# A two-pass order for a planned kernel: the first layout's times, shifted for 116 groups of operations, rank the second, and ten groups of keys are added in one VectorE sum

## The chip, the cores and the metric

The kernel runs on one core of one Trainium2 chip. The metric is the device time of one execution in microseconds. The instructions of each engine (TensorE, shown as PE for products and PEld for weight loads; VectorE as DVE; ScalarE as ACT; GpSimd as POOL; SyncE as SP, which issues the transfers) stand in one fixed order, written when the kernel is built, and an engine executes them strictly in that order. What another engine or a transfer has to deliver is waited for at the instruction that needs it.

## The reference

Four residual blocks on x of 2048 rows by 640 columns: attention, MLP, attention, MLP, both pairs with the same weights.

```python
def A(x, wqkv, wo):                    # 32 heads of 20 columns
    q, k, v = split(x @ wqkv)
    idx = pos[:, None] - arange(8) * 2 # 8 keys per row, every second row back
    logits = where(idx >= 0, einsum(q, k[idx]) * 20 ** -0.5, -1e9)
    return einsum(softmax(logits), v[idx]) @ wo
def B(x, w1, b1, w2, b2):              # 640 -> 1536 -> 640
    return gelu(layernorm(x) @ w1 + b1) @ w2 + b2
x = x + A(layernorm(x)); x = x + B(layernorm(x))
x = x + A(layernorm(x)); x = x + B(layernorm(x))
```

## The kernel before

**Units.** The 2048 rows are cut into four units of 512 rows (even and odd rows apart, since keys stand two rows back), four tiles of 128 rows each. Two layers make eight units, n = 0 to 7. A float32 factor is held as two float16 parts, the high part and what is left, and a product of two such factors is three TensorE products (`PASS`). The left-over part costs one subtraction: `yl` for layer norm rows, `lo` for weights, `hlo` for the MLP's hidden values, `ol` for attention's result. ScalarE makes the high part before it (`yh`, `hi`, `hhi`, `oh`).

**A unit's path.** Layer norm (`layernorm`); rows split and transposed by a DMA into `yT`; QKV products (`qkv`, for units 4 to 7 `qkv7`, with seven instead of eight half-size products, in steps P1 to P7 with ScalarE copies between them); results written to DRAM (`spill`) and read back as windows (`fetch`); attention on VectorE (`attention`); its output transposed and multiplied by wo (`project`); a second layer norm; the MLP (`mlp`, 12 blocks e of 128 hidden columns: `hp` is the first product of a block, `outh` and `out` the second). The last two units' MLP is done together (`pair`).

**Attention on VectorE.** A unit has four groups of 8 heads, so there are 32 groups G. A group runs products of q and its 8 keys (`qk`, L1004, 5120 elements a partition), the sum over a head's columns (`lg`, L1009), mask, maximum, difference, exponent on ScalarE, sum (`s`), reciprocal (`rc`), weights (`at`), products with v (`pv`, L1026), and then the sum over the 8 keys in three additions of 2560, 1280 and 640 elements (`ad`, twice L1031, and `o`, L1034).

**Weights.** While unit 0's MLP runs, the 12 blocks of W1 and W2 are loaded (`st`, L531), scaled and split (`sc` L539, `hi` L540, `lo` L541) and stored for later units (`mw`, L551). W2's blocks stand in three buffers c2: a block takes one for the loaded float32 values and one for its two parts, which is free again when the block's products and its store are done. Units 4 to 7 need combined blocks of the QKV weights, built by `factors` (`fr` loads, L764; `fs` four differences, L772; `fh`, `fl`).

**The planner.** `Plan.add` collects some 3,700 operations with an engine, a cost, a priority, what they need and give, and the buffers they use. `Plan.run` lays them out in time: of the operations that are ready on an engine, the one with the least key (earliest start, then priority, then number) is next. The result is only the order; the chip sets the times. An operation added with `either` (rather than `dve`) may go to GpSimd instead of VectorE, but only where the plan has VectorE in an `lg` sum: the planner opens such a stretch (`open_`) at every `lg` and puts the operation there if it fits. `HOLD` keeps an `either` operation from VectorE for some time, so that such a stretch may come. The lines that set a pick:

```python
key = (max(t - o["wait"], clock[e] + 0.05, (o["born"] + o["hold"]) * (e == "dve" and o["hold"] > 0)), o["prio"], o["n"])
```

Of the kernel before, what the change touches and what calls it, by code (L numbers as in the profile page):

```python
# [37 lines left out]
FAST = ([0, 1, 2], [0, 1])  # L38
# [29 lines left out]
PAIRS = ("qk", "pv", "ad", "o", "sub", "at", "hlo", "yl", "xb", "ol", "wq", "lo", "lm")  # L68

HOLD = {'lo': 0, 's': 2, 'hlo': 0, 'b': 0, 'xb': 20, 'ol': 12, 'ol3': 0}  # L70
# [3 lines left out]
QKV_AT = (-500, -499, 0, 9, 9, 6, 4, 0)  # L74
ROWS_AT = (-500, -199, -198, -17, -16, -15, -94, -13)
INNER_AT = (-150, -149, -698, -147, -146, -145, -694, -43)
HOLD_A = (0, 6, 6, 12, 12, 6, 0, 12)
PREP_AT = 0
# [7 lines left out]
class Plan:  # L86
# [12 lines left out]
    REACH = 0.75  # L99
# [11 lines left out]

    def __init__(self, slots):
        self.ops = []
        self.free = {pool: [(0.0, i) for i in range(n)] for pool, n in slots.items()}
        self.users = {}
        self.slot = {}
        self.since = {}
        self.last = {}
        self.turn = {}
        self.line = {}  # L120
        self.turns_up = {}

    def add(self, eng, dur, prio, emit, need=(), give=(), use=(), table=None, move=None, lazy=False, wait=None,
# [3 lines left out]
                 wait=self.PATIENCE * (eng == "dve" and prio < -200) if wait is None else wait)  # L127
        self.ops.append(o)
        for u in use:
            if u not in self.users and u[0] in self.ORDERED and u not in self.line.setdefault(u[0], []):  # L130
                self.line[u[0]].append(u)
            self.users[u] = self.users.get(u, 0) + 1

    def run(self):
        when = {}
# [115 lines left out]
        while len(order) < total:  # L251
            best = None
            for e, ops in ready.items():
                pick = None
                for o in ops:
# [3 lines left out]
                    key = (max(t - o["wait"], clock[e] + 0.05, (o["born"] + o["hold"]) * (e == "dve" and o["hold"] > 0)), o["prio"], o["n"])  # L259
# [66 lines left out]
def sliding_dilated_then_mlp_kernel(  # L326
# [121 lines left out]
    def either(n, hold, prio, emit, need=(), give=(), use=(), aside=None):  # L448
        dve(n, prio, emit, need, give, use, aside=aside or 0.12 + n / 500.0, hold=hold)
# [218 lines left out]
    def sums_of_rows(n, prio, name, yk, lk, col):  # L668
# [4 lines left out]
        for b in range(2):  # L673
# [9 lines left out]
            def sum1(yks=yks):  # L683
                y1 = tile_of(*yks[1])
                nc.vector.tensor_add(y1[:, :KQ], y1[:, :KQ], y1[:, KQ:2 * KQ])

            def sums(yks=yks):
                y0, y1 = (tile_of(*k) for k in yks)
                nc.vector.tensor_sub(y0[:, :KQ], y1[:, :KQ], y0[:, :KQ])
# [55 lines left out]
    def flat(t):  # L745
        return t.rearrange("p k a c -> p (k a c)")
# [864 lines left out]
```

## Time and profile before

| | |
|---|---|
| median of 3 runs | 1133.01 us (1132.67 to 1134.62) |
| the profiled execution's own time | 1132.52 us |
| its span, first to last instruction | 1130.7 us |
| mean granted TensorE clock | 0.998 |
| TensorE products | 6536, busy 1118.3 us, 99% of the span |
| VectorE | busy 1050.9 us, 93% |
| ScalarE, GpSimd | busy 672.8 us (59%) and 144.6 us (13%) |
| moved by DMAs | 250.91 MB |

The time of a run is the span and some 1.8 us around it (1132.52 less 1130.7). A busy share says how much of the span an engine had an instruction in work, not whether that work set the end; a matmul's end is modelled in these records, so TensorE's pace is read from the starts of groups of equal products.

### The profile page before, as it was taken

The numbers are of one execution on the slowest core, as the hardware profiler recorded it, in microseconds if no ns is written. First come the engines' busy times: TensorE is split into PE (matmuls) and PEld (weight loads), VectorE is DVE, ScalarE is ACT, GpSimd is POOL, SyncE is SP. The second block draws the span as 40 slices with busy tenths as digits, with TensorE's granted clock in tenths as the row PEclk, the third lists the DMA queues.
The fourth block names the chain that finished last, engine by engine and source line by source line (L and its number), as shares of the span: only waits on it lengthen the run. The fifth ranks groups of instructions, "written<-read, shape, count | busy, mean of one in ns | idle before, by whom it ended". The sixth has DMA issues, their size and how long they took to land.

```text
span 1130.7 us, 17031 instructions
## 1 busy us (share of the span) xinstructions
PE 1118.3 (99%) x6536; PEld 602.0 (53%) x6536; DVE 1050.9 (93%) x885; ACT 672.8 (59%) x1241; POOL 144.6 (13%) x109
## 2 busy tenths in 40 slices
PE   9999999999999999999999999999999999999998
PEld 6444455445545455455545554446445555654476
DVE  7899999999999999999999999999999998768972
ACT  6558446566946556565735675378644843858630
POOL 1102103101012013120211200112100300000000
PEclk9999999999999999999999999999999999999999
DMA  9998787689997798688785859768898766695202
GB/s 310 316 323 235 217 224 174 236 304 274 292 320 239 192 288 240 198 222 223 221 274 181 214 166 269 245 224 199 184 297 239 216 196 171 182 258 154 65 24 70
DMA packets 262605, 250.91 MB, mean 222 GB/s; under 512 B 154412, under 2 KB 219260, under 8 KB 262524
## 3 DMA queue, kind: packets, MB, share of 16 engines
q1 hardware_dynamic: 262524, 249.83, 75.6%
q8 instruction: 51, 0.84, 0.3%
q14 instruction: 30, 0.25, 0.1%
HBM read 161.49 MB, written 52.64 MB: 189 GB/s over the span
## 4 chain that ended last, share of the span: by engine, by line
PE 68%; DVE 19%; issue 5%; DMA 4%; SPq 2%; ACT 2%; POOL 0%; DVEq 0%; ACTq 0%; POOLq 0%
PE acc L1151 15%; PE ps L1130 15%; PE ps L910 13%; PE ps L838 10%; PE ps L1063 6%; PE acc L1332 3%; DVE pr L1031 3%; PE ps L1367 3%; DVE pr L1026 3%; DVE pr L1004 3%; DVE sm L1009 2%; PE ps L1332 2%; DMA c<-in_B_w_dram 1%; DVE w L654 1%; DVE act L1141 1%
## 5 line engine op out<-in xcount | busy, mean ns | idle before, releaser
L1151 PE MATMUL acc<-c,act 128*128 128x512 f16 (+1 forms) x1728 | 250.4, 300 | 3.2 <-ACT c L540 2.8
L1130 PE MATMUL ps<-yT,c 128*128 128x512 f16 x1080 | 243.7, 379 | 0.1
L1151 PEld LDWEIGHTS <-act 128*128 128x128 f16 x1728 | 136.8, 98 | 114.7 <-issue 5.3
L910 PE MATMUL ps<-wq,yT 128*128 128x480 f16 (+1 forms) x990 | 196.5, 360 | 0.6 <-ACT wq L506 0.5
L1004 DVE TENSOR_TENSOR pr<-qk 128x5120 f32<-128x5120 f32 x32 | 175.1, 5473 | 1.5 <-DMA qk<-spill 1.2
L1026 DVE TENSOR_TENSOR pr<-sm,v 128x5120 f32<-128x5120 f32 x32 | 175.7, 5490 | 0.8
L1009 DVE TENSOR_REDUCE sm<-pr 128x256 f32<-128x5120 f32 x32 | 175.1, 5472 | 0.0
L1130 PEld LDWEIGHTS <-c 128*128 128x128 f16 x1080 | 103.6, 98 | 122.0 <-DVE c L541 0.6
L910 PEld LDWEIGHTS <-yT 128*128 128x128 f16 x990 | 95.3, 98 | 99.1 <-issue 0.7
L1031 DVE TENSOR_TENSOR pr<-pr 128x2560 f32<-128x2560 f32 x64 | 137.7, 2151 | 0.1
L1063 PE MATMUL ps<-wo,yT 128*128 128x320 f16 x960 | 132.0, 299 | 0.0
L838 PE MATMUL ps<-wq,yT 128*128 128x480 f16 x528 | 112.6, 366 | 1.8 <-ACT ps L856 1.8
L1063 PEld LDWEIGHTS <-yT 128*128 128x128 f16 x960 | 93.8, 98 | 37.7
L1136 ACT ACTIVATE act<-ps,b 128x512 f32<-128x512 f32 x72 | 49.2, 684 | 83.4 <-PE ps L1130 83.0
L847 ACT ACTIVATE ev<-ps 128x480 f32<-128x480 f32 x96 | 52.8, 566 | 72.6 <-PE ps L838 67.2
L621 POOL TENSOR_TENSOR ln<-ln,half 128x2 f32<-128x2 f32 (+1 forms) x32 | 52.4, 1638 | 315.2 <-ACT ln L618 315.2
L838 PEld LDWEIGHTS <-yT 128*128 128x128 f16 x528 | 51.1, 98 | 55.8 <-issue 2.3
L930 ACT ACTIVATE ev<-ps 128x480 f32<-128x480 f32 x64 | 36.3, 569 | 73.0 <-PE ps L910 72.5
L838 PE MATMUL ps<-wq 128*128 128x480 f16 x336 | 71.8, 366 | 1.1 <-ACT ev L847 1.1
L1042 POOL TENSOR_TENSOR ohl<-w,ohl 128x640 f16<-128x640 f32 x18 | 25.3, 1403 | 296.6 <-DVE sm L1024 56.1
L1139 ACT ACTIVATE act<-act 128x512 f16<-128x512 f32 x72 | 44.8, 622 | 21.2 <-PE acc L1151 20.9
L838 PEld LDWEIGHTS <-wq 128*128 128x128 f16 x336 | 32.6, 98 | 35.7 <-issue 1.5
(224 smaller groups left out, 1323.4 us busy)
## 6 DMA issues: line engine op xcount, KB each, us to landing
c<-mw SPq DMA_DIRECT2D x126, 320.0 KB, 3.6
spill<-ev SPq DMA_DIRECT2D x64, 480.0 KB, 4.1
qk<-spill SPq DMA_DIRECT2D x32, 880.0 KB, 5.9
v<-spill SPq DMA_DIRECT2D x32, 880.0 KB, 4.9
qk<-spill SPq DMA_DIRECT2D x32, 320.0 KB, 3.3
c<-in_B_w_dram SPq DMA_DIRECT2D x24, 320.0 KB, 4.9
mw<-c SPq DMA_DIRECT2D x24, 320.0 KB, 4.6
pr<-in_B_w_dram SPq DMA_DIRECT2D x24, 320.0 KB, 3.9
```

What stands on the lines that cost most here:

```text
L621: pool(0.6, prio, lambda t0=t0, t1=t1: nc.gpsimd.tensor_tensor(col(2)[:, t0:t1], col(2)[:, t0:t1], half[:, t0:t1], op=OP.pow), need=[("vr" ...
L838: nc.tensor.matmul(ps, r(x_, j), w[:, j, y_], start=start and i == 0, stop=i == len(todo) - 1, skip_group_check=True)
L847: act(C, -400 + n, lambda: nc.scalar.activation(to(), tile_of(*bank)[:, :C].rearrange("p (a c) -> p a c", a=3), AF.Copy, scale=1.0 / WS), ...
L910: nc.tensor.matmul(ps, transposed(yk)[:, a * KD + k, t * P:(t + 1) * P], wq[:, g, k, b, i0 * GC:i1 * GC], start=first and j == 0, stop=las ...
L1004: nc.vector.tensor_mul(pr.rearrange("p w t c -> p w (t c)"), w[:, HALO + m:HALO + 2 * m].rearrange("p t c -> p (t c)")[:, None, :].to_broa ...
L1009: dve(E, G - 0.7, lambda: nc.vector.tensor_reduce(by_key(), heads(), axis=AX.X, op=OP.add), need=[("qk", G)], give=[("lg", G)], use=[*pk, sk])
L1026: dve(E, G - 0.85, lambda: nc.vector.tensor_mul(heads(), by_key()[:, :, :, None].to_broadcast([P, W, m * GH, DH]), windows(tile_of(*vw), [ ...
L1031: dve(m * w * GC, G - 0.9, lambda w=w: nc.vector.tensor_add(pr[:, 0:w], pr[:, 0:w], pr[:, w:2 * w]), need=[last], give=[("ad", G, w)], use=vk)
L1063: nc.tensor.matmul(tile_of(*pk)[:, :D // 2], transposed(yk)[:, a * KD + k, t * P:(t + 1) * P], wo[:, b, k, c * D // 2:(c + 1) * D // 2], s ...
L1130: nc.tensor.matmul(tile_of(*pk)[:, :nt], tile_of(*ck)[:, a, k * P:(k + 1) * P], transposed(yk)[:, c * KD + k, t0 * P:t1 * P], start=i == 0 ...
L1151: nc.tensor.matmul(accs[k][:, c0:c0 + n], tile_of(*hk)[:, a, (i - t0) * P:(i - t0 + 1) * P], tile_of(*wk)[:, c, w0:w0 + n], start=first, s ...
L1332: nc.tensor.matmul(tile_of(*to(i))[:, :HALF], hl()[:, a, i * P:(i + 1) * P], row(c), start=start and (a, c) == PASS[0], stop=(a, c) == PAS ...
```

## The change

**Two layouts.** `run` now calls `lay` twice. The first layout is made as before, by priorities. `rank` keeps each operation's time in it (`first`). In the second layout the rank of an operation is that time, plus a shift for its name from the table `SHIFT`: 116 names, of one operation (`'yl a 1 0'`) or of a family (`'lo m 9'`), shifted by between -206.5 and 90.5. For held operations the hold becomes "not before 3 us ahead of its rank".

**More for GpSimd.** The row sums of `sums_of_rows` (L685, and its second part), the differences of `factors` (L772) and the addition `ea` of `qkv7` (L870) become `either` operations. The list `PAIRS` and some numbers (`HOLD`, `QKV_AT`, `ROWS_AT`, `INNER_AT`, `HOLD_A`, `PREP_AT`, `REACH`) are changed. `FAST` loses its second entry: two tiles of unit 1's layer norm go from VectorE (`bn_stats`) to ScalarE.

**One sum over the keys.** For the ten groups marked in `ONCE` (1, 2, 6, 7, 9, 10, 13, 21, 30, 31) the three additions over keys become one VectorE reduction of 5120 elements to 640, read with the eight keys innermost, 2560 bytes apart (`ow`). The planner opens a stretch for GpSimd at an `ow` too.

```diff
-FAST = ([0, 1, 2], [0, 1])
+FAST = ([0, 1, 2],)
...
+SHIFT = {
+    'P7 4': -2, 'XP1 0 1': 3, 'XP1 2 1': 20, 'ad 15': 10, 'ad 17': -7, 'ad 25': 2, 'ad 25 2': 3, 'at 6': -10, 'c1 P1 3': -5, 'e 26': -17, 'fl 1': 9.5,
...
     def run(self):
+        self.lay()
+        if SHIFT:
+            self.rank()
+            self.lay()
+        return self.order
+
+    def rank(self):
+        for o in self.order:
+            o["first"] = o["at"]
...
+            if "first" in o:
+                o["rank"] = o["first"] + sum(SHIFT.get(k, 0.0) for k in set(o["key"]))
+                o["until"] = o["rank"] - self.EARLY if o["hold"] > 0 else 0.0
...
-                    key = (max(t - o["wait"], clock[e] + 0.05, (o["born"] + o["hold"]) * (e == "dve" and o["hold"] > 0)), o["prio"], o["n"])
+                    held = (o["until"] if "first" in o else o["born"] + o["hold"]) if e == "dve" and o["hold"] > 0 else 0.0
+                    key = (max(t - o["wait"], clock[e] + 0.05, held), o["rank"], o["n"])
...
-                if kind == "lg":
+                if kind in ("lg", "ow"):
                     open_.append((t, t + d))
...
-            dve(KQ, prio, sum1, need=[("y", name, 2 * b + 1)], give=[("rs", name, b)], use=held)
+            either(KQ, HOLD["rs"], prio, sum1, need=[("y", name, 2 * b + 1)], give=[("rs", name, b)], use=held)
...
+        if ONCE[G]:
+            dve(E, G - 0.9, lambda: nc.vector.tensor_reduce(
+                ot().rearrange("p t c -> p (t c)"), pr.rearrange("p w t c -> p (t c) w"), axis=AX.X, op=OP.add),
+                need=[last], give=[("ow", G), ("o", G)], use=[*vk, ok])
+        else:
...
```

The program has the same 6536 products and the same transfers on SP's queue as before, in another order. VectorE has 65 instructions fewer, GpSimd 34 more, and ScalarE 13 more, among them two more changes of its function table there and back. Ten `tensor_reduce` stand for thirty additions; moved from VectorE to GpSimd, net, are 12 of the `hlo` (L1141), 7 of the `lo` (L541), 6 `ea` (L870), 4 `yl` of units 4 to 7 (L714), one `fs` of four differences (L772), 4 first row sums (L685) and 2 other `yl` (L654); back to VectorE come 3 additions of b2 (L660) and 1 `ol` (L1042).

Three places in the order follow. Line numbers of the changed kernel differ: L579 is the weight load L531, L812 is L764, L1176 is L1123, L704 is L656, L1010 is L962, L599 is L551, L589 is L541, L1194 is L1141, L1095 is L1042, L1079 the new reduction.

SP's queue, before, from the loads for `factors` (L764) over the loads of W2's blocks 9 (into c22) and 10 (into c20); c10 to c12 are the buffers of W1's blocks, v0 and qk0 the attention's windows, yT1 transposed rows:

```order
L764 DMA wq_101<-in_A_wqkv_dram 128x3x160 x4
L1123 DMA c10_76<-mw00_110 128x1280
L962 DMA v0_68<-spill01_135 128x1760
L551 DMA mw18_130<-c20_79 128x1280
L531 DMA c22_81<-in_B_w2_dram 128x640
L551 DMA mw011_121<-c12_78 128x1280
L1123 DMA c11_77<-mw01_111 128x1280
L656 DMA_TRANSPOSE yT1_73<-w3_85 128x10x128
L1123 DMA c12_78<-mw02_112 128x1280
L531 DMA c20_79<-in_B_w2_dram 128x640
```

The same stretch of SP's queue now, to the load of block 10 (into c21):

```order
L1010 DMA v0_68<-spill01_135 128x1760
L599 DMA mw010_120<-c10_76 128x1280
L704 DMA_TRANSPOSE yT1_73<-w4_86 128x10x128
L704 DMA_TRANSPOSE yT1_73<-w3_85 128x10x128
L579 DMA c22_81<-in_B_w2_dram 128x640
L599 DMA mw18_130<-c21_80 128x1280
L1176 DMA c10_76<-mw00_110 128x1280
L599 DMA mw011_121<-c11_77 128x1280
L1176 DMA c12_78<-mw01_111 128x1280
L579 DMA c21_80<-in_B_w2_dram 128x640
L1176 DMA c11_77<-mw02_112 128x1280
```

The four loads for `factors` that stood 4 rows ahead of block 9 come 25 rows behind block 10 now; four others of the same kind, which came long before, have moved to 9 to 14 rows ahead of block 9. The load of block 10 stands ahead of the third W1 block (c11 now, c12 before) instead of behind it.

VectorE before, from W2's block 9 (`lo`, into c21) to block 10 (`lo`, into c22), with attention group 8's sums and group 9's softmax between:

```order
L541 TENSOR_TENSOR c21_80<-c22_81,c21_80 128x640
L654 TENSOR_TENSOR w2_84<-w4_86,w2_84 128x640
L654 TENSOR_TENSOR w3_85<-w1_83,w3_85 128x640
L1018 TENSOR_TENSOR sm1_88<-sm1_88 128x256
L1031 TENSOR_TENSOR pr_95<-pr_95 128x1280
L786 SCALAR_TENSOR_TENSOR wq_101<-wq_101 128x3x480
L1022 TENSOR_REDUCE sm1_88<-sm1_88 128x32
L1034 TENSOR_TENSOR w4_86<-pr_95 128x640
L541 TENSOR_TENSOR c22_81<-c20_79,c22_81 128x640
```

Both now stand on GpSimd (the first and the fourth of these rows), with hidden values and an attention result between them:

```order
L589 TENSOR_TENSOR c20_79<-c22_81,c20_79 128x640
L1194 TENSOR_TENSOR act_66<-act_66 128x512
L1095 TENSOR_TENSOR ohl0_75<-w2_84,ohl0_75 128x4x160
L589 TENSOR_TENSOR c22_81<-c21_80,c22_81 128x640
L708 TENSOR_TENSOR xf_65<-xf_65,b2_104 128x640 x2
```

The two subtractions that the products of blocks 9 and 10 need have left VectorE's queue, and the planner has put all four of these GpSimd rows beside the `lg` sum of group 10.

VectorE before, the three sums over group 9's keys (L1031 twice and L1034), and what stood between them:

```order
L1031 TENSOR_TENSOR pr_95<-pr_95 128x2560
L1013 TENSOR_TENSOR sm0_87<-sm0_87,mask_109 128x256
L1031 TENSOR_TENSOR pr_95<-pr_95 128x1280
L1141 TENSOR_TENSOR act_66<-act_66 128x512
L1016 TENSOR_REDUCE sm0_87<-sm0_87 128x32
L1034 TENSOR_TENSOR w1_83<-pr_95 128x640
```

VectorE now, from group 9's weights and products with v to its one sum (L1079):

```order
L1072 TENSOR_TENSOR sm1_88<-sm1_88 128x256
L1074 TENSOR_TENSOR pr_95<-sm1_88,v0_68 128x5120
L834 SCALAR_TENSOR_TENSOR wq_101<-wq_101 128x480
L589 TENSOR_TENSOR c20_79<-c21_80,c20_79 128x640
L1079 TENSOR_REDUCE w1_83<-pr_95 128x640
```

Three instructions, between which others could stand, have become one.

At the start of SP's queue the second tile of x now stands ahead of the first block of the QKV weights (it stood behind it), and on TensorE the transposes of the second tile now stand ahead of the first product.

More of the change, by code (lines that the diff above doesn't have):

```diff
@@ L98 @@
     AHEAD = 3.0
-    REACH = 0.75
+    REACH = 0.5
     LAND = 0.9
@@ L110 @@
     ORDERED = ("ax", "ts", "qk", "v", "yT", "o", "ohl", "c1", "c2", "hh", "h32", "ev", "raw")
+    EARLY = 3.0
     def __init__(self, slots):
         self.ops = []
[L114 to L119, printed above, removed]
+        self.slots = slots
+        self.count = {}
         self.line = {}
-        self.turns_up = {}
     def add(self, eng, dur, prio, emit, need=(), give=(), use=(), table=None, move=None, lazy=False, wait=None,
@@ L767, in factors, with combine @@
                         need=[*plain(1), *gone], give=[("fr", p, j, i)], use=[ak], packet=4 * GC)
[L769 removed]
+                def combine(eng, raw=raw):
                     b11, b12, b21, b22 = raw
                     for to, a, b in ((b11, b12, b11), (b12, b22, b12), (b22, b22, b11), (b21, b21, b22)):
[L772 to L774 removed]
+                        eng.tensor_sub(to, a, b)
+                either(4 * C, HOLD["fs"], PREP_AT, combine, need=[("fr", p, j, i) for i in range(4)], give=[("fs", p, j)], use=[ak], more=0.2, aside=0.5 + 4 * C / 500.0)
                 for i, n in enumerate((3, 1)):
```

72 lines of the change are left out of this document (44 added, 28 removed), and 12 rows, old and new, of the table SHIFT.

## The prediction

> **What bounds the kernel now.** I read the page's busy rows first, then who TensorE waits for, then TensorE's order of time around its longest wait, then the other engines there.
>
> ```profile
> span 1130.7 us, 17031 instructions
> PE   1118.3 (99%) x6536; PEld 602.0 (53%) x6536; DVE 1050.9 (93%) x885; ACT 672.8 (59%) x1241; POOL 144.6 (13%) x109
> ```
>
> TensorE is the bound: 6536 products in 1118.3 of 1130.7 us, and the change has the same products. What it can win is the time in which TensorE stands or runs slowly, and the waits say how much that is.
>
> ```profile
> PE acc L1151 <- ACT c L540: 2.8, 1, 2.8
> PE ps L838 <- ACT ps L856: 1.8, 2, 1.2
> PE ps L838 <- ACT ev L847: 1.1, 2, 0.6
> PE ps L1367 <- ACT qk L1439: 0.6, 1, 0.6
> PE ps L910 <- ACT wq L506: 0.5, 1, 0.5
> PE acc L1151 <- DVE c L541: 0.4, 1, 0.4
> PE acc L1332 <- ACT act L1339: 0.4, 1, 0.4
> ```
>
> The columns are total, times and longest. All but the fifth, which is at the start, lie inside the run: 7.1 us. Two of them, 3.2 us, are one place, where W2's block 10 is late:
>
> ```profile
> 303.24 3.20 PE L910 MATMUL ps<-wq,yT 128*128 128x480 f16 x15
> 306.28 3.42 PE L1151 MATMUL acc<-c,act 128*128 128x512 f16 x24
> 312.51 0.43 PE L1151 MATMUL acc<-c,act 128*128 128x512 f16 x2 [2.81 <-ACT c L540]
> 313.37 4.78 PE L1151 MATMUL acc<-c,act 128*128 128x512 f16 x22 [0.43 <-DVE c L541]
> ...
> 327.70 3.42 PE L1151 MATMUL acc<-c,act 128*128 128x128 f16 x24
> 330.96 6.64 PE L1130 MATMUL ps<-yT,c 128*128 128x512 f16 x30
> ...
> 300.00:325.00 25.00, 21.76 (x120) 10.78 (x118) 24.76 (x20) 17.01 (x24) 4.26 (x3) 0.93 1.05 307
> 690.00:705.00 15.00, 13.83 (x77) 6.84 (x76) 14.93 (x10) 8.53 (x14) 0.00 (x0) 1.00 1.03 288
> ```
>
> Start, duration, products. In the last two rows the third number from the end is the granted clock. Here 24 products take 3.26 us at full pace (327.70 to 330.96), so 22 should take 2.99. Behind the wait they took 4.78: 1.8 us more, and the stretch's clock is 0.93. So this one place costs 2.81 + 0.43 + 1.8 = 5.0 us. The other waits inside the run are 3.9 us (1.8 + 1.1 + 0.6 + 0.4); if every one went, the span would be 1130.7 - 8.9 = 1121.8. The second view of the limits is VectorE, which is nearly full for most of the run:
>
> ```profile
> 50.00:950.00 900.00, 893.80 (x5138) 469.32 (x5136) 886.17 (x614) 543.48 (x1016) 132.59 (x90) 1.00 0.80 235
> ```
>
> In these 900 us VectorE (third column of work) is busy for 886.2 and idle for 13.8. It doesn't hold TensorE up by itself, 0.4 us of wait is all it causes, but little more work fits in.
>
> **The change, term 1: block 10 (taken as -4.3 us, bounds -5.0 and 0).** Why block 10 was late, by the rows of SP, ScalarE and VectorE:
>
> ```profile
> 304.46 0.37 SPq L531 DMA_DIRECT2D c<-in_B_w_dram  x1
> ...
> 307.28 1.40 ACT L784 ACTIVATE wq<-wq 128x1440 f16<-128x1440 f32 x1
> 308.69 1.28 ACT L1020 ACT_TABLE_LOAD   x1
> 310.31 0.72 ACT L539 ACTIVATE c<-c 128x640 f32<-128x640 f32 x1
> 311.23 0.60 ACT L784 ACTIVATE wq<-wq 128x480 f16<-128x480 f32 x1 [0.20 <-DVE wq L786]
> 311.74 0.72 ACT L540 ACTIVATE c<-c 128x640 f16<-128x640 f32 x1
> ...
> 312.49 0.83 DVE L541 TENSOR_TENSOR c<-c,c 128x640 f16<-128x640 f32 x1 [0.24 <-ACT c L540]
> c<-in_B_w_dram SPq DMA_DIRECT2D x24, 320.0 KB, 4.9
> ```
>
> The load was issued at 304.46, 1.2 us after block 8's products ended at 303.24 and freed its buffer. At the page's median of 4.9 us (last row) it landed near 309.4. ScalarE was then in a table load, from 308.69 to 309.97, and in the exponent behind it, and scaled the block only from 310.31; another `fh` (0.60) came between scaling and splitting; the subtraction followed at 312.49. TensorE meanwhile had one QKV tile (3.04 us, 303.24 to 306.28) and block 9's products (3.2): 6.3 us of work against the 10 us that the block took from 303.24 to 313.3.
>
> In the new order TensorE has two QKV tiles between the end of block 8 and block 9, so 3.04 x 2 + 3.26 = 9.3 us of work. On ScalarE both the `fh` of this half and the exponent stand behind the block's splitting. The chain becomes 1.2 (to the issue) + 4.9 (landing) + 0.72 + 0.72 + the subtraction, now on GpSimd, 1.40 (row below) + some 0.3 between engines, from the gaps in these rows: 9.2 + 0.1 to 0.8 for a load that lands as late as the nearest ones. Against 9.3 that leaves a wait of 0 to 0.7; I take 0.7, and no slow stretch behind it, since the stretch from 690, which holds the wait of 1.2 at L838, has a clock of 1.00. -5.0 + 0.7 = -4.3. If the load is as late as before plus the slower subtraction, most of the 5.0 stays: that is the bound at 0.
>
> **Term 2: TensorE's other waits inside the run (0, bounds -3.9 and +3.9).** Three of the four kinds wait for a ScalarE copy between two steps of one bank (P1 to P2, P6 to P7 and their likes in `pair`). Each of these couplings exists in the new order too, with other ScalarE work ahead of it; what is won at one is lost at another unless a row says otherwise, and none does. ScalarE also gets more: two more table changes there and back, 4 x 1.28 = 5.1 us, and unit 1's two layer norm tiles. It is busy 59%: cost 0 on the path, within these bounds. Unit 1's transposed rows are the one thing that moves late:
>
> ```profile
> 48.06 0.37 SPq L936 DMA_DIRECT2D spill<-ev  x1
> 48.48 4.25 SPq L656 DMA_TRANSPOSE yT<-w  x2
> ...
> 60.27 0.38 SPq L936 DMA_DIRECT2D spill<-ev  x1
> ```
>
> Their first issue moves from well ahead of the store at 48.06 to behind it (unit 0's third group). Two of them hold the queue for 4.25, and with a landing like that of the weights (4.9, above) the second is there at 57.2. TensorE begins unit 1 about a copy (0.6) and a lag ahead of the store of unit 0's last tile, at 60.27: 59.5. It fits, with 2 us to spare.
>
> **Term 3: VectorE's and GpSimd's work (0 on the path).**
>
> ```profile
> L1009 DVE TENSOR_REDUCE sm<-pr 128x256 f32<-128x5120 f32 x32 | 175.1, 5472 | 0.0
> L1031 DVE TENSOR_TENSOR pr<-pr 128x2560 f32<-128x2560 f32 x64 | 137.7, 2151 | 0.1
> L1034 DVE TENSOR_TENSOR w<-pr 128x640 f32<-128x640 f32 x32 | 26.3, 821 | 0.7
> L1026 DVE TENSOR_TENSOR pr<-sm,v 128x5120 f32<-128x5120 f32 x32 | 175.7, 5490 | 0.8
> L1016 DVE TENSOR_REDUCE sm<-sm 128x32 f32<-128x256 f32 x32 | 13.2, 413 | 0.1
> L1141 DVE TENSOR_TENSOR act<-act 128x512 f16<-128x512 f32 x63 | 42.9, 684 | 1.4 <-ACT act L1139 0.9 <-PE acc L1151 0.5
> L541 DVE TENSOR_TENSOR c<-c,c 128x640 f16<-128x640 f32 x18 | 14.4, 820 | 4.5 <-ACT c L540 4.5
> L870 DVE TENSOR_TENSOR ev<-ev,ev 128x960 f32<-128x960 f32 x16 | 18.4, 1148 | 0.2 <-ACT ev L847 0.2
> L1042 POOL TENSOR_TENSOR ohl<-w,ohl 128x640 f16<-128x640 f32 x18 | 25.3, 1403 | 296.6 <-DVE sm L1024 56.1 <-DVE w L654 40.2 <-DVE sm L1022 40.1
> L1141 POOL TENSOR_TENSOR act<-act 128x512 f16<-128x512 f32 x9 | 10.4, 1158 | 35.7 <-ACT act L1139 35.7
> L621 POOL TENSOR_TENSOR ln<-ln,half 128x2 f32<-128x2 f32 (+1 forms) x32 | 52.4, 1638 | 315.2 <-ACT ln L618 315.2
> ```
>
> The last number before the second bar is the mean of one in ns. The three additions cost 2 x 2.151 + 0.821 = 5.12 us a group. The one sum reads 5120 elements, as L1009 does in 5.47: +0.35 us each, +3.5 for ten. No row reads with 2560 bytes between elements, so this is bounded: below by the three additions it replaces (5.12), above by the nearest row that sums eight values to one, L1016, 413 ns for 256 elements, twenty times that for 5120: 8.26. I take 5.47, since L1009 has the same length and L1016's 413 ns is mostly what any row of 256 elements costs.
>
> Leaving VectorE: 12 x 0.684 + 7 x 0.820 + 6 x 1.148 = 20.8 us, and some 9 us of smaller moves and of unit 1's statistics, which I leave unquoted. So VectorE loses about 30 and gains 3.5. On GpSimd a subtraction takes 1.40 beside a VectorE sum (L1042), and GpSimd is busy 13%. The price is 0 as long as TensorE stays the bound; what gets earlier is attention, by up to 26 us, and its results wait in buffers.
>
> **Term 4: the start (+0.3, bounds -0.3 and +1.3).** The first weights are loaded one transfer later, and the split of the second weight part stands ahead of ScalarE's copies of the first transposed tile, so the first product starts later than now (the 0.5 us wait at L506 belongs to this place); in return the second tile's transposes are done before it. The ends: that wait gone less 0.2, and one load of 320 KB at the 307 GB/s of the row for 300 to 325 (1.04) and 0.3 of lag.
>
> **Sum.** -4.3 + 0 + 0 + 0.3 = -4.0 against the profiled execution's 1132.5, which is 1128.5; the median of the runs is 0.5 above that execution, so I predict 1129.0, 0.35% faster. Its own range is 1125.8 to 1130.7.
>
> **Rivals.**
>
> *The small waits go too.* With VectorE ahead, ScalarE's inputs come earlier, and the second layout may place its copies better. All but 0.5 us of term 2 gone: 1129.0 - 3.4 = 1125.6. For it: none of these waits is over 1.2 us, about one ScalarE operation that could stand elsewhere. Against it: the couplings are as many as before.
>
> *The win is lost at the next link.* GpSimd's operations are placed beside a VectorE sum. One that misses it gets behind VectorE's two-input work: L621, two elements a partition, takes 1638 ns on average here. Block 10's subtraction is the fourth GpSimd operation beside one sum of 5.47 us (1.40 + 1.16 + 1.40 + 1.40 = 5.4), so any late one misses, and behind that sum come a product of 5.49 and block 11's subtraction. Each costs 1 to 3 us, and a wait near 3 brings the slow stretch of 1.8 back: +3 to +4.8 on the forecast, 1132.0 to 1133.8, no change that a measurement can tell (it tells about 0.2%, 2.3 us).
>
> *The sum over keys reads slowly (the slower side).* Place: the ten reductions. If each element takes two of the steps in which L1009 takes one, a sum costs 2 x 5.47 = 10.9 us, 5.8 more than the three additions, 58 us in all. VectorE loses about 30 elsewhere and has 13.8 idle; the 14 us left, at least, go on its path, and as its order can't be changed it becomes the bound around groups 6 to 13: 1133 + 14 = 1147, up to 1133 + 28 = 1161 if the idle time can't be used; 1152. It decides from 5.12 + 3.0 = 8.1 us a sum on, where the ten eat the 30. For it: no row shows such a read. Against it: L1009 and L1026 take 5.47 and 5.49 whatever they broadcast or step over. [...]
>
> **How the numbers follow.** Forecast 0.55, small waits too 0.12, lost at the next link 0.18, slow sum 0.10, another new wait of 4 us or more (unit 1's rows, or unit 4's first product, whose rows hang on two more moves to GpSimd; 1135 to 1139) 0.05. Faster by over 0.2%: 0.55 + 0.12 = 0.67; same 0.18; slower 0.15. The range takes in the first three cases and the near part of the last: from 1124.0 (all 8.9 us of waits gone from the median) to 1135.0, leaving 0.13 out; the slow sum lies outside.
>
> **What the next profile would show.** Right: TensorE's wait for c at L540 under 1 us and no stretch with a clock below 0.97; the ten sums at 5.4 to 5.6 us; VectorE's busy time 20 to 30 us less; GpSimd near 190 us; attention's last sum over keys some 20 us earlier. Wrong: sums over 8 us and VectorE's share above 93%; a wait for a GpSimd subtraction at L1151; first product later than 9.5 us; new waits at L838 of over 1 us each.

## The result, and the profile after

The changed kernel takes 1171.04 us (median of 4 runs, 1168.78 to 1172.32) against 1132.87 (1132.67 to 1134.62) before: 1.0331 times the time, 95% interval 1.0312 to 1.035, so 38 us slower where 4 us faster were predicted. First the span and the busy times of its page:

```profile
span 1170.5 us, 17016 instructions
PE 1128.9 (96%) x6536; PEld 604.5 (52%) x6536; DVE 1067.8 (91%) x820; ACT 683.5 (58%) x1258; POOL 189.9 (16%) x143
```

TensorE has the same 6536 products and is now busy for 96% of the span instead of 99%: it waits, and its busy time is 10.6 us longer than before for the same work. VectorE has 65 instructions fewer and 16.9 us more work. Its groups, by shape, of the changed kernel (the last number before the second bar is the mean of one, in ns):

```profile
L1057 DVE TENSOR_REDUCE sm<-pr 128x256 f32<-128x5120 f32 x32 | 175.2, 5474 | 0.1
L1079 DVE TENSOR_REDUCE w<-pr 128x640 f32<-128x5120 f32 x10 | 90.3, 9032 | 0.0
L1084 DVE TENSOR_TENSOR pr<-pr 128x2560 f32<-128x2560 f32 x22 | 62.0, 2817 | 0.0
...
L1084 DVE TENSOR_TENSOR pr<-pr 128x1280 f32<-128x1280 f32 x22 | 32.7, 1485 | 0.1
...
L1087 DVE TENSOR_TENSOR w<-pr 128x640 f32<-128x640 f32 x22 | 18.0, 817 | 0.4
```

The new sum (L1079) takes 9.03 us. The three additions that it replaces take 2.82 + 1.49 + 0.82 = 5.12, and the sum of the same 5120 elements over a head's columns (L1057) 5.47. So ten groups cost 39.1 us more VectorE work, and the work moved to GpSimd and ScalarE takes 22 away. The waits of TensorE that follow, without those at the start (total, times, longest):

```profile
PE ps L1116 <- DMA yT<-ohl: 10.4, 2, 5.7
PE ps L886 <- ACT ev L895: 8.7, 5, 3.0
PE ps L886 <- ACT ps L904: 5.4, 2, 5.1
PE ps L1183 <- DVE c L589: 4.3, 1, 4.3
PE acc L1204 <- DVE act L1194: 2.1, 1, 2.1
PE acc L1204 <- DVE xf L1248: 1.9, 1, 1.9
...
PE acc L1204 <- DVE c L589: 1.1, 2, 0.6
```

These are 33.9 us, where before had 7.1 in all. The rest is mostly the 10.6 us of longer busy time: slow stretches behind the longer waits. One place shows how a late sum reaches TensorE. VectorE's order of time, and then TensorE's:

```profile
253.41 9.05 DVE L1079 TENSOR_REDUCE w<-pr 128x640 f32<-128x5120 f32 x1
262.50 5.49 DVE L1052 TENSOR_TENSOR pr<-qk 128x5120 f32<-128x5120 f32 x1
267.91 0.82 DVE L589 TENSOR_TENSOR c<-c,c 128x640 f16<-128x640 f32 x1
```

```profile
268.78 4.42 PE L1183 MATMUL ps<-yT,c 128*128 128x512 f16 x13 [4.26 <-DVE c L589]
273.04 2.28 PE L1204 MATMUL acc<-c,act 128*128 128x512 f16 x15
```

The busy times of this stretch (in order PE, weight loads, VectorE, ScalarE, GpSimd, then the granted clock):

```profile
262.00:275.00 13.00, 8.63 (x44) 3.73 (x43) 12.86 (x11) 7.31 (x11) 0.32 (x1) 0.87 0.60 204
```

The subtraction for a weight block (L589) needs nothing of attention, but stands behind group 7's sum and group 8's products with the keys. The sum is 3.6 us longer than it was planned, the subtraction that much later, and TensorE stands for 4.26 us. Then 13 products take 4.26 us (268.78 to 273.04), where the prediction's row of 30 such products (6.64 us) gives 2.9; the granted clock of these 13 us is 0.87.

The kernels of the experiments. Each ratio is taken over all executions, against executions of the kernel before that were run along with them, and need not be that of the medians:

| kernel | median, us | ratio to before (95%) | what it is |
|---|---|---|---|
| near_read | 1134.28 | 1.0009 (0.9999 to 1.0019) | changed, fast read |
| adds_there | 1157.26 | 1.0217 (1.0199 to 1.0235) | changed, additions in the sums' places |
| old_order | 1193.14 | 1.0521 (1.0506 to 1.0536) | before, ten sums |
| pairs | 1133.43 | 1.0000 (0.9991 to 1.0009) | changed, other layout of the products |
| far_early, far_late | 1151.85, 1153.03 | 1.0163 (1.0148 to 1.0179), 1.0176 (1.0159 to 1.0193) | five of the ten slow |
| near_swap | 1133.34 | 1.0002 (0.9994 to 1.0011) | near_read, two loads later |
| block10 | 1133.29 | 1.0005 (0.9996 to 1.0014) | before, block 10 earlier |
| block10_rows | 1133.57 | 1.0001 (0.9992 to 1.001) | and unit 1's rows |
| pairs_rs | 1132.75 | 0.9996 (0.9986 to 1.0005) | pairs, one row sum back |
| pairs_four | 1131.35 | 0.9980 (0.9971 to 0.9989) | pairs, four steps moved |
| no_once | 1160.97 | 1.0237 (1.022 to 1.0254) | changed, no single sums, laid out anew |

### The profile page after: what moved, and what is told of

The parts are those of the page before. It is cut to its first block, busy times and chain, and to the rows that moved or that the text cites. A ratio compares the mean times of both kernels' runs of the same rounds, so it can differ in the third digit from the quotient of the medians.

```text
span 1170.5 us, 17016 instructions
## 1 busy us (share of the span) xinstructions
PE 1128.9 (96%) x6536; PEld 604.5 (52%) x6536; DVE 1067.8 (91%) x820; ACT 683.5 (58%) x1258; POOL 189.9 (16%) x143
## 5 line engine op out<-in xcount | busy, mean ns | idle before, releaser
L1057 DVE TENSOR_REDUCE sm<-pr 128x256 f32<-128x5120 f32 x32 | 175.2, 5474 | 0.1
L1116 PE MATMUL ps<-wo,yT 128*128 128x320 f16 x960 | 136.9, 305 | 10.4 <-DMA yT<-ohl 10.4
L886 PE MATMUL ps<-wq,yT 128*128 128x480 f16 x528 | 116.2, 373 | 9.1 <-ACT ps L904 5.4
L1084 DVE TENSOR_TENSOR pr<-pr 128x2560 f32<-128x2560 f32 (+1 forms) x44 | 94.6, 2151 | 0.1
L1079 DVE TENSOR_REDUCE w<-pr 128x640 f32<-128x5120 f32 x10 | 90.3, 9032 | 0.0
L1092 ACT ACTIVATE ohl<-w 128x640 f16<-128x640 f32 x32 | 23.4, 732 | 61.2 <-DVE w L1079 43.4
L1095 POOL TENSOR_TENSOR ohl<-w,ohl 128x640 f16<-128x640 f32 x17 | 23.8, 1402 | 209.7 <-DVE sm L1072 34.7
```

The source lines that it names most:

```text
L886: nc.tensor.matmul(ps, r(x_, j), w[:, j, y_], start=start and i == 0, stop=i == len(todo) - 1, skip_group_check=True)
L1057: dve(E, G - 0.7, lambda: nc.vector.tensor_reduce(by_key(), heads(), axis=AX.X, op=OP.add), need=[("qk", G)], give=[("lg", G)], use=[*pk, sk])
L1079: dve(E, G - 0.9, lambda: nc.vector.tensor_reduce(ot().rearrange("p t c -> p (t c)"), pr.rearrange("p w t c -> p (t c) w"), axis=AX.X, op= ...
L1084: dve(m * w * GC, G - 0.9, lambda w=w: nc.vector.tensor_add(pr[:, 0:w], pr[:, 0:w], pr[:, w:2 * w]), need=[last], give=[("ad", G, w)], use=vk)
L1116: nc.tensor.matmul(tile_of(*pk)[:, :D // 2], transposed(yk)[:, a * KD + k, t * P:(t + 1) * P], wo[:, b, k, c * D // 2:(c + 1) * D // 2], s ...
```

## The experiments: what makes the sum slow

**The read alone.** Edit of near_read:

```diff
-ot()..., pr.rearrange("p w t c -> p (t c) w"), axis=AX.X, op=OP.add
+ot()..., pr.rearrange("p w t c -> p (w t c)").rearrange("p (x w) -> p x w", w=W), axis=AX.X, op=OP.add
```

> The changed kernel with the same instructions in the same order; only each of the ten sums adds eight neighbouring values of its 5120 instead of the eight keys, 2560 bytes apart (so it leaves out the sum over the keys; the time alone is read). Theory A, the distance between the read elements is the whole cause: the sums take 5.4 to 5.6 us instead of 9.03, and the run takes 1125 to 1132 us, the waits of 2 to 6 us for results behind those sums are gone. Rival B, the new order itself is worse (moves to GpSimd, shifted ranks) and the slow sums only add to it: the sums take 5.5 us, the run stays above 1145 us. Rival C, a reduction from 5120 to 640 elements takes 9 us whatever it reads: sums of 9.0 us, 1171 us.

Measured: the ten sums take 5.48 us each and the run 1134.28 us. So the order is not what lost 38 us (B falls), nor the form of the instruction (C). But the run is 2.3 us above the upper end that A gave: with sums as fast as planned the new order is worth nothing. That second question is taken up below.

**Distances by themselves** (strides):

> A program of its own, of VectorE instructions on one array of 5120 values a partition, each three times, with nothing beside them (it computes nothing of the reference; the durations alone are read): sums of 8 values that stand 4, 8, 16, 32, 64, 256 and 2560 bytes apart, a sum of 4 values 2560 bytes apart over 2560, additions of 5120 elements that read both inputs, one input, or write with such a step, and the plain ones. [...] Rival A2, the far distance itself: the cost grows from 16 to 2560 bytes. Rival C, the form of the reduction: 9.0 at all distances. For additions: with a far read 9 us or more if reading is what is slow, 5.5 if only reductions are; with far writing 5.5 if writing is free of it, which would allow the products with v to be written with the eight keys side by side.

Its VectorE groups; L32 reads its eight values 4 bytes apart, L35 8, L38 16, L50 2560; of the additions L68 is plain, L64 writes 32 bytes apart:

```profile
L64 DVE TENSOR_TENSOR to<-pr 128x5120 f32<-128x5120 f32 x3 | 28.2, 9386 | 0.0
...
L38 DVE TENSOR_REDUCE w<-pr 128x640 f32<-128x5120 f32 x3 | 27.7, 9220 | 0.0
...
L50 DVE TENSOR_REDUCE w<-pr 128x640 f32<-128x5120 f32 x3 | 26.3, 8766 | 0.0
...
L32 DVE TENSOR_REDUCE w<-pr 128x640 f32<-128x5120 f32 x3 | 16.5, 5499 | 0.0
L68 DVE TENSOR_TENSOR to<-pr 128x5120 f32<-128x5120 f32 x3 | 16.5, 5489 | 0.0
L35 DVE TENSOR_REDUCE w<-pr 128x640 f32<-128x5120 f32 x3 | 16.5, 5485 | 0.0
```

A step from 8 to 16 bytes, and none up to 2560 (9.3 at 32 bytes, 8.7 to 8.8 from 64 on): 1.6 to 1.7 times the time, for additions and reductions, for reading (8.86 for an addition with one input read 2560 bytes apart) and writing (9.39 at 32 bytes). So A2 and C fall. A step of 12 bytes was not run.

**Two values side by side** (pairs). In the ten groups the products with v are written as pairs of columns, each pair's eight keys side by side:

```diff
+heads(last): pr.rearrange("p w t c -> p (w t c)").rearrange("p (x w s) -> p w x s", w=W, s=2)
-ot()..., pr.rearrange("p w t c -> p (t c) w")
+ot()...rearrange("p (x s) -> p x s", s=2), pr.rearrange("p w t c -> p (w t c)").rearrange("p (x w s) -> p x s w", w=W, s=2)
```

> The changed kernel in its order, computing the same; in the ten groups the products with v are written so that two neighbouring columns of each of the eight keys stand side by side (8 bytes, then 64 bytes on), and the sum reads its eight values 8 bytes apart instead of 2560. By the durations of the single reads (8 bytes apart 5.49 us, 16 bytes and more 8.7 to 9.3, writing single values 32 bytes apart 9.39): theory A1, what counts is whether two accesses in a row fall into the same 16 bytes, for writing too: sums 5.5 us, products with v 5.5 us, run 1132 to 1136 us, as with the neighbouring read (1134.3). Rival A3, writing pays for every jump: products with v 7 us or more in the ten groups, run 1145 to 1170 us.

VectorE's groups in it: L1081 writes the products as before, L1078 as pairs, L1088 is the sum:

```profile
L1081 DVE TENSOR_TENSOR pr<-sm,v 128x5120 f32<-128x5120 f32 x22 | 120.8, 5490 | 0.6
...
L1078 DVE TENSOR_TENSOR pr<-sm,v 128x5120 f32<-128x5120 f32 x10 | 54.9, 5490 | 0.2
L1088 DVE TENSOR_REDUCE w<-pr 128x640 f32<-128x5120 f32 x10 | 54.8, 5478 | 0.0
```

Writing 8 bytes and jumping 64 costs nothing (5.49 us either way), the sum has its planned time (5.48), and the run takes 1133.43, as before: the whole loss (1171.04 less 1133.43 is 37.6 us) hangs on the distance, and a layout removes it. A3 falls. The times are those that A1 gave; of its 16 bytes the runs show that a step of 8 is fast and one of 16 slow, and no more.

**The sum in the old order** (old_order: `o` of the ten groups becomes the sum, both `ad` are left out):

> The kernel before in its own order; in the same ten groups (1, 2, 6, 7, 9, 10, 13, 21, 30, 31) the third addition is replaced by the one sum over the keys and the first two are left out. Theory A, the sum costs the same anywhere: 9.03 us each, 3.9 us more than the three additions, 39 us of VectorE work of which at most 14 us find idle time; TensorE waits for some 25 to 35 us: 1157 to 1172 us. Rival E, the sum is slow only in the new order, beside GpSimd's operations on the same memory: 5.5 us each here and 1132 to 1137 us.

The sums take 8.95 us each, so E falls. The run takes 1193.14, 59 us more for 38 us of work: above the range of A. The edit explains a part of this, for it puts the whole sum in the place of the last addition. At 403.50 a sum of 8.76 us stands where before had an addition of 0.82 (at 377.64). ScalarE's copy of its result waits for it, the copy that TensorE needs stands behind that one, and TensorE waits 12.45 us (0.61 at that place before). A second such wait, at 745, is 8.01 us. In the new order the same sums cost 37.6 us.

**What each one costs.** `ONCE[G] and G not in FAR` (FAR stands for the five groups) chooses the layout in pairs:

> The kernel with pairs of columns side by side in the groups 10, 13, 21, 30 and 31, whose sums take 5.5 us, and the far read in the groups 1, 2, 6, 7 and 9, whose sums take 9.0: 17.8 us more of VectorE work than with pairs in all ten. Threshold theory: that is less than the 20 us by which VectorE's work is smaller than before, so 1133 to 1137 us. Theory I, no threshold: VectorE's order is fixed and it is full up to 650 us, so each sum's 3.55 us delays all that stands behind it, and TensorE waits for the next of its operands there: 17.8 and some 2 to 3 us of slow stretches, 1148 to 1155 us.

> The reverse: far reads in the groups 10, 13, 21, 30 and 31. Threshold theory: 1133 to 1137 us. Theory I: the sums of groups 10 and 13 lie where VectorE is full and cost their 3.55 us each; that of group 21 lies where VectorE has some idle time in the changed kernel (94 of 100 us from 650 to 750), and those of 30 and 31 where it has more (80 of 100), but the last unit's rows for wo wait for both, so 3.55 to 7 more: 1143 to 1153 us.

Against pairs, five early sums cost 18.4 us and five late ones 19.6, for 17.8 us of work; together 38.0, where all ten cost 37.6. There is no threshold: 17.8 us is less than the 19.4 by which VectorE's work fell from before to near_read (1050.9 to 1031.5), and it was paid in full. Theory I holds, with far_late at the upper edge of its range. What a single sum costs was not measured.

**Additions in the sums' places** (adds_there):

> The changed kernel in its order, with the three additions (2560, 1280 and 640 elements) standing in the place of each of the ten sums. Theory A: the three take 5.1 us, nearly what the order was planned with (5.4), so the run comes out as with the neighbouring read, 1125 to 1132 us. Rival D, GpSimd's operations need a VectorE reduction beside them: beside two-input additions they get slower (1.40 us subtractions to 2 us and more), are late in their turn, and the run takes 1135 to 1145 us.

The run takes 1157.26 us, above both ranges. VectorE's groups in it, ten additions of 1280 and ten of 640 elements:

```profile
L1079 DVE TENSOR_TENSOR pr<-pr 128x1280 f32<-128x1280 f32 x10 | 23.8, 2379 | 0.3
...
L1080 DVE TENSOR_TENSOR w<-pr 128x640 f32<-128x640 f32 x10 | 14.4, 1435 | 0.4
```

Elsewhere these take 1.49 and 0.82. With the first addition (2.92 on the mean) the three take 6.73 us instead of 5.12 (the 6.2 in the expectation below is too low). GpSimd is slower too: its ten `lo` subtractions (L589) take 2.00 us on the mean, 1.41 in near_read, and TensorE waits 3.6 and 3.3 us for two of them. So D has the mechanism, and its price was too low. To see the pairing alone (beside):

> A program of its own (it computes nothing of the reference; the durations alone are read): three GpSimd subtractions of 640 elements, as for the left-over parts, beside nothing, beside a VectorE sum with near reads, beside one with far reads, beside a product of 5120 elements, and beside the three additions. Theory D, GpSimd and VectorE's two-input instructions hold each other up, a reduction doesn't: 1.40 us each beside nothing and beside both sums, the sums stay at 5.5 and 8.8 us; 1.9 us or more beside the product and the additions, whose 5.1 us become 6 or more (in the changed kernel with the additions put in the sums' places they took 6.2 on the mean). Rival: the losses there came from the order, and the pairs measured alone show 1.40 and 5.1.

Its order of time, VectorE and GpSimd: beside the near sum, the far sum, a product, the first addition, and (last row) nothing; the rows of L48 are the three subtractions, and the row at 45.44 is the third addition:

```profile
12.81 5.48 DVE L31 TENSOR_REDUCE w<-pr 128x640 f32<-128x5120 f32 x1
12.98 4.34 POOL L48 TENSOR_TENSOR half<-src,half 128x640 f16<-128x640 f32 x3 [12.54 <-DVE src L51]
...
18.26 8.79 DVE L34 TENSOR_REDUCE w<-pr 128x640 f32<-128x5120 f32 x1
18.42 4.35 POOL L48 TENSOR_TENSOR half<-src,half 128x640 f16<-128x640 f32 x3 [1.10 <-DVE src L51]
...
27.04 5.48 DVE L37 TENSOR_TENSOR to<-pr 128x5120 f32<-128x5120 f32 x1
27.19 9.52 POOL L48 TENSOR_TENSOR half<-src,half 128x640 f16<-128x640 f32 x3 [4.42 <-DVE src L51]
...
36.81 2.82 DVE L40 TENSOR_TENSOR to<-pr 128x2560 f32<-128x2560 f32 x1
36.98 6.85 POOL L48 TENSOR_TENSOR half<-src,half 128x640 f16<-128x640 f32 x3 [0.27 <-DVE src L51]
...
45.44 1.90 DVE L42 TENSOR_TENSOR w<-to 128x640 f32<-128x640 f32 x1
...
50.33 4.34 POOL L48 TENSOR_TENSOR half<-src,half 128x640 f16<-128x640 f32 x3 [0.27 <-DVE src L51]
```

Three subtractions take 4.34 us beside either sum, as beside nothing. Beside a product they take 9.52, and beside the first addition 6.85: 4.34 and nearly the whole of the VectorE instruction. It is the first of the three that stands until that instruction ends: beside the product, the 9.52 us less the 2.88 of two subtractions (beside the far sum) leave it 6.6, an estimate from these rows. This bears out D. The third addition took 1.90 instead of 0.82 behind a GpSimd operation that had begun (the three beside the last two additions begin at 44.09 and take 5.97), so the holding goes both ways. So the one sum has a use: it is a window for GpSimd. Read far it costs 3.9 us more than the three additions, read as pairs 0.35, and in this order the additions in its place cost 24 us more than pairs (1157.26 against 1133.43).

**No single sums** (no_once, `ONCE` all 0):

> The changed planner with all its shifts and moves, but with three additions in all 32 groups, and the order laid out anew for that. GpSimd's operations then stand beside the first sum of a group only. If the slow sums are the whole loss, it takes what the order is worth, 1130 to 1136 us; since the shifts were set for another layout, a late operand of 2 to 5 us in some places is as likely: up to 1145 us. Above 1150 us the moves to GpSimd themselves would be at fault.

The run takes 1160.97 us. TensorE's longest wait in it is one of 9.6 us for transposed rows, from 108 us on; the next is 3.7. By the expectation this would be the fault of the moves to GpSimd, but ten windows less and shifts made for another layout can't be told apart here: it is inconclusive.

## The experiments: why fast sums win nothing

In near_read block 10 is as the prediction said. GpSimd's, SP's and TensorE's order of time:

```profile
308.56 1.41 POOL L589 TENSOR_TENSOR c<-c,c 128x640 f16<-128x640 f32 x1
...
305.27 7.24 SPq L704 DMA_TRANSPOSE yT<-w  x2
...
306.89 6.68 PE L1204 MATMUL acc<-c,act 128*128 128x512 f16 x48
316.25 8.27 PE L1183 MATMUL ps<-yT,c 128*128 128x512 f16 x30 [2.68 <-DMA yT<-w]
```

The subtraction ends at 309.97 and the products of blocks 9 and 10 run in one piece to 313.6. Then TensorE waits for the rows of unit 1's second layer norm, whose last two transposes hold SP until 312.5. TensorE gets on at 316.25. In the kernel before it began the same unit's products at 317.99, just behind block 10:

```profile
317.99 7.29 PE L1130 MATMUL ps<-yT,c 128*128 128x512 f16 x33
```

So near_read is 1.7 us ahead there. But its 30 products take 8.27 us, where a row of 30 takes 6.64 elsewhere: the slow stretch has moved behind the new wait and eats the 1.6 to 1.7 us.

Whether these rows are late differs between executions of the same order on SP. In pairs, the kernel that computes the right sums, the two transposes took 5.90 us instead of 7.24 and there is no wait for them. TensorE there:

```profile
312.86 6.64 PE L1193 MATMUL ps<-yT,c 128*128 128x512 f16 x30
...
320.59 3.36 PE L1214 MATMUL acc<-c,act 128*128 128x128 f16 x23 [0.80 <-DVE c L589]
...
393.43 3.61 PE L886 MATMUL ps<-wq,yT 128*128 128x480 f16 x9 [2.28 <-ACT ps L904]
```

It begins unit 1's products 5.1 us ahead of the kernel before, then waits for block 11 (0.80) and at 391 for ScalarE (2.28), and runs slowly behind that (9 products in 3.61 us; 1.98 in near_swap, below). The gain of block 10 was real and was lost at later links.

**Rows ahead of loads** (near_swap: `inq` and `ink` of group 11 behind both transposes):

> The changed kernel with the neighbouring read (ten sums add eight neighbouring values instead of the keys; the time alone is read), and on SP's queue the two loads of group 11's windows (1.2 MB together) put behind the two transposes of unit 1's second layer norm instead of ahead of them. With the neighbouring read alone TensorE's wait for W2's block 10 was gone, but it then waited 2.7 us at 313.4 for these transposed rows and ran slowly behind that: 4.4 us at one place. Theory F, the gain of block 10 was real and was lost to these rows, which stand behind the loads: the wait goes, 1129.5 to 1131.5 us. Rival G, at this place the DMA engines are full (share 0.98 to 1.08 from 300 to 325 in both), so the rows land no earlier, or another transfer is late instead: 1133 to 1136 us.

The wait went, and TensorE was 3 us further. Then it waited 1.03 us for block 11 at 319.6 and 2.3 us at 391. GpSimd, ScalarE, TensorE there:

```profile
391.67 0.73 POOL L733 TENSOR_TENSOR w<-w 128x256 f32<-128x256 f32 x1
...
392.43 0.74 ACT L760 ACTIVATE w<-w 128x640 f16<-128x640 f32 x1 [1.48 <-POOL w L733]
...
393.68 1.58 PE L886 MATMUL ps<-wq,yT 128*128 128x480 f16 x7 [2.28 <-ACT ps L904]
```

The row sum L733, which the change gave to GpSimd, had its input at 385.7. It stands behind an attention result (L1095, at 390.31), and both were laid into one window, the sum of group 12 that begins at 390.1. ScalarE waits for the row sum, and its copy between P1 and P2, which TensorE needs, stands behind that. In near_read TensorE came there 3.6 us later and waited 0.9. The median is 1133.34, no change: rival G, though the waits that came back are for VectorE and ScalarE, not for transfers.

**Term 1 by itself, in the old order** (block10: `sc`, `hi` of block 10 ahead of `e` 9; `o` 8, `lo` of block 10 ahead of `fl`; block10_rows: unit 1's last transpose ahead of two stores as well):

> The kernel before in its own order, with block 10's scaling and splitting on ScalarE moved ahead of group 9's exponent and its table load, and block 10's subtraction and group 8's last addition on VectorE ahead of one subtraction for the combined weights. Term 1 of the prediction by itself: block 10 is ready 1.3 to 1.8 us earlier, the wait of 3.2 us shrinks to 1.5 and the slow stretch of 1.8 us with it: if nothing else is late, 1129.5 to 1131 us. Theory F, the next products need unit 1's transposed rows, whose last transpose was issued at 311.4 and held SP until 313.4, so they can't start much before 317 (317.99 now): 1132 to 1133.5 us, no change.

> As the one before, and on SP's queue the last transpose of unit 1's rows moved ahead of a store of 480 KB and one of 320 KB. Theory F: rows and block 10 are now both earlier, by some 1.5 us, and the run gains that and part of the slow stretch: 1129.5 to 1131.5 us. Rival G, the transfers are bound by the DMA engines there, the rows land when they did: 1132 to 1133.5 us, as with block 10 alone.

TensorE in block10, then in block10_rows:

```profile
310.24 0.43 PE L1151 MATMUL acc<-c,act 128*128 128x512 f16 x2 [0.29 <-ACT c L540]
311.51 3.15 PE L1151 MATMUL acc<-c,act 128*128 128x512 f16 x22 [0.84 <-DVE c L541]
316.62 8.75 PE L1130 MATMUL ps<-yT,c 128*128 128x512 f16 x32 [1.96 <-issue]
```

```profile
314.42 9.88 PE L1130 MATMUL ps<-yT,c 128*128 128x512 f16 x45
...
336.72 3.53 PE L1151 MATMUL acc<-c,act 128*128 128x512 f16 x23 [1.48 <-DVE xf L1195]
```

In block10 the wait of 3.2 us has become 1.1, and the slow stretch is gone from this place (22 products in 3.15 us, not 4.78). Unit 1's products then begin at 316.62 instead of 317.99. The profile names nothing that they waited for ("issue"). That it was their rows, as F said, is borne out by block10_rows, where the last transpose stands earlier and they begin at 314.42. In block10 they are slow: 32 take 8.75 us, where the pace of block10_rows (45 in 9.88) gives 7.0, and block 11's products begin at 328.01, not ahead of before (327.70). In block10_rows TensorE is 3.6 us ahead of before at 314; by 337 three small waits (0.31, 0.56 and 1.48) have taken 2.35 us of it back, and at 380 nothing is left (380.65 against 380.25). The medians are 1133.29 and 1133.57, no change.

**One and four steps on pairs** (pairs_rs: that row sum on VectorE; pairs_four: also the loads of group 11 and of group 24's v later, `su3` of unit 6 ahead of `e` 22):

> The kernel with pairs of columns side by side, with one GpSimd operation back on VectorE: the row sum of unit 4's second pair of tiles (256 elements, 0.42 us), which GpSimd could start only when the VectorE sum of group 12 began, 4 to 6 us after its input was there; ScalarE waited for it and TensorE, 2.3 us at 391, for ScalarE. Theory H, that turn costs the 2.3 us: the wait goes and the run takes 1130.5 to 1132 us. Rival G, what is won there is waited for at a later place: 1132.5 to 1134 us, no change.

> As the one before, and three more steps at the places where TensorE waited longest: the loads of group 11's windows behind unit 1's transposed rows, unit 6's copy for P7 ahead of group 22's exponent and its table load (0.9 us at 671), the load of group 24's v behind two stores (1.7 us at 738). If the waits are each of its own, 2.3 + 0.9 + 1.7 + up to 1 for what follows slowly are won: 1128 to 1130 us, faster than both kernels. Rival G, the transfers and VectorE, which is busy for 595 of 600 us to 650, set the pace and each removed wait comes back behind it: 1132 to 1134 us.

In pairs_rs the wait at 391 is gone from the trace, but the median, 1132.75, is within the uncertainty of no change. The profiled execution was the slowest of twelve (1137.57), and in it the wait for unit 1's rows is back (2.74 us). pairs_four is 1131.35 us, 0.9980 of before (0.9971 to 0.9989): the only kernel here that beats the kernel before, by 2.0 us, less than half of what the sum of its waits had given. The busy times of its page:

```profile
PE 1117.7 (99%) x6536; PEld 602.1 (53%) x6536; DVE 1031.3 (91%) x821; ACT 683.9 (61%) x1258; POOL 185.8 (16%) x142
```

and the stretch from 50 to 650 us, of the kernel before and of pairs_four:

```profile
50.00:650.00 600.00, 595.50 (x3381) 310.61 (x3379) 593.19 (x418) 362.75 (x680) 97.50 (x65) 1.00 0.82 243
50.00:650.00 600.00, 595.24 (x3406) 313.09 (x3405) 596.52 (x387) 370.54 (x702) 127.76 (x91) 1.00 0.83 244
```

There TensorE is busy for 595.2 and VectorE for 596.5 of 600 (595.5 and 593.2 before): both are full. With some 20 us less work in all, VectorE is not less full there; what it saves shows only later (from 650 to 950 it is busy for 280.5 us, before for 293.0). My reading, by the places above, is that a step that brings TensorE forward brings it to an operand that VectorE, GpSimd or a transfer delivers at its old time. Which of the four steps won the 2 us was not told apart.

## Why the prediction was wrong

**What bounds.** Right that TensorE bounds and that only its waits can be won. Wrong that each can be won by itself (1130.7 - 8.9 = 1121.8): behind block 10 stood unit 1's rows, 2.7 us later in near_read, and where these came in time (pairs), block 11 and the copy at 391.

**Term 3, the step that failed.** The prediction priced the one sum at 5.47 us, "since L1009 has the same length", within bounds of 5.12 and 8.26, and put its cost on the path at 0. It measured 9.03, outside the bounds, and with it VectorE's work rose by 16.9 us instead of falling by 26.5; the run lost 38 us. The upper bound was twenty times a row of 256 elements that lie side by side. The term compared by length, and what counted was how the elements lie. What it held against the rival, that L1009 and L1026 take 5.47 and 5.49 us whatever they step over, was no test: both read neighbouring values one after another. No row of the kernel before had such a read, so neither price rested on a measured one, and 0.10 for that rival was too little.

**The slow-sum rival** had the place and the sign, but its price was low in form: it let VectorE's freed 30 us pay first and came to 1147 to 1161 (1171 measured), deciding from 8.1 us. Far_early and far_late show that the sums are paid in full, with no freed time to take them up; by theory I that is so because the order is fixed. The relief was also 19.4 us with fast sums, where the term had 26.5.

**Term 1.** The mechanism was right: in after, near_read and pairs no wait for block 10 stands there. The 4.3 us were not kept: they went to the next links (with fast sums the ratio to before is 1.0009 and 1.0000). So even with a sum of 5.47 us the forecast of 1129.0 would have missed by some 4 us, though inside its range. The rival "lost at the next link" gave 1132.0 to 1133.8; pairs measured 1133.43. Its mechanism, a GpSimd operation that is late for its window, is near to the one at 391 us; at 316 us it is transposes instead.

**Term 2.** The waits inside the run other than the one for rows are 4.9 us in near_read against 3.9 before, within the bounds; in pairs they are 8.9, 5.0 more and outside them. Unit 1's first rows fitted, as said.

**Term 4.** Not settled: executions of the same start differ by over 1 us in TensorE's busy time to 30 us (27.05 in after, 26.72 in pairs, 28.16 in pairs_four; 28.02 before), nearly as much as the term's bounds. Most start later than before, as the term has it.

**The signs.** GpSimd at 190 us came true; sums over 8 us, a first product later than 9.5 us (10.0) and waits of over 1 us at the ScalarE copies (3.0 and 5.1) came true from the list for "wrong". VectorE's share didn't rise above 93%, as the span grew with it. Attention's last sum over keys did not come 20 us earlier even with fast sums: it ends at 950.9 in near_read, the last addition at 953.1 before.

## What to carry over

Price a VectorE instruction by the bytes between elements it touches one after another, not only by its count: here steps of 4 and 8 bytes were fast (5.50 and 5.49 us for 5120 values), steps of 16 bytes and more took 1.6 to 1.7 times as long (8.70 to 9.39), and a layout in pairs put that right (5.48). In this fixed order longer instructions on an engine that is nearly full were paid in full (18.4 and 19.6 us for 17.8 of work), even though its total work fell. And a wait is worth only the distance to the next late operand: before counting it, look up when what follows it is ready.

## What the runs showed of the hardware

VectorE's time steps up between 8 and 16 bytes from one value it reads to the next (5.49 and 9.22 us for 5120 values); writing single values 32 bytes apart takes 9.39. GpSimd loses nothing beside a VectorE reduction, even a slow one (4.34 us for three subtractions beside nothing and beside the near sum, 4.35 beside the far one), and stands for nearly the whole of a two-input instruction (9.52 beside a product of 5.48). The length of a wait alone doesn't say whether TensorE runs slowly behind it: at one place, after 2.28 us each time, 9 products took 3.61 us in pairs (granted clock 0.88 from 386 to 400 us) and 1.98 in near_swap (1.00).
